# The last 64-token group of an attention and mixer kernel in two column parts, with its stores in parts on both queues

## The chip, the cores and the metric

The kernel runs on one core of a Trainium2 chip. The metric is the device time of one execution in microseconds (us), the median of several runs; less is better. Engines are named as the profile names them: PE is TensorE (PEld its weight loads), DVE is VectorE, ACT is ScalarE, POOL is GpSimd, SP is SyncE, which here only issues transfers; a q behind a name is that engine's instruction queue. A name such as L891 is a line of the kernel before.

## The reference

For each of 8 batches, 12 heads, 448 tokens and head dimension 64, sigmoid attention; its output, heads side by side, is a matrix x of 448 tokens by 768 columns, and goes through a mixer:

```python
scores = scale * np.matmul(q, k.transpose(0, 1, 3, 2)) - np.log(S)
attn = 1.0 / (1.0 + np.exp(-scores))
x = np.matmul(attn, v)                       # then (B, S, H * D)
h = np.maximum(xt @ w_tok1, 0.0) @ w_tok2    # xt: x with tokens last
u = x + h.transpose(0, 2, 1)
h2 = np.maximum(u @ w_ch1, 0.0) @ w_ch2
return u + h2
```

Inputs and output are float32; the kernel computes its products from float16 operands into float32 sums.

## The kernel before

The schedule is written out by hand: instructions go to the engines in the order of the Python code, and waits are put between them where data or buffers demand it. Batches overlap: while the scores and values of one batch are computed, the channel products of the batch before are done in between. At the end only the channel products of batches 6 and 7 are left, and then the last group of batch 7.

Tokens are taken as position p = 0 to 63 and residue j = 0 to 6 (token 7 p + j), so a batch is seven groups of 64 tokens, by residue. Residues 0 to 5 make three pairs of 128 tokens. The seventh residue, 64 tokens, is alone. In the second channel product, `h2` (the hidden values, 12 blocks of 128 channels by 448 tokens) is the stationary operand and `c2` (the weights, 12 blocks of 128 by 768 columns) the moving one; the 768 columns are done as two halves of `DH` = 384.

The pairs of 128 tokens of batches 6 and 7 go through `ch2_seven`: seven products of six matmuls in place of eight (L814), each sum added to an output tile by DVE (L841, three columns blocks of 128 at a time). When a pair is ready, `store` (L621) sends its two 64-token rows, 192 KB each; for batch 7 the first goes out from SP and the second from ACT, for batch 6 both from SP.

The last group is `ch2_last(B - 1)`, called in four portions of three blocks by `pieces_last`. The 64 tokens fill only half of the array's columns, so the two halves of the output columns, g = 0 and 1, are done side by side: g = 0 into partitions 0 to 63 of one PSUM bank, g = 1 into partitions 64 to 127 of another. Twelve pairs of matmuls of 384 columns (L891) are followed by three pairs of 128 columns (L902), which add u: `ut(b, db)` is u with its columns on the partitions, so a matmul with the identity turns it over into the sum. Then DVE copies g = 0 (L914) and ACT copies g = 1 (L912) into the tile `o` of `last_tile`, and each half, 96 KB, is stored by a queue of its own, SP and ACT (L923).

`un[b]` is u with tokens on the partitions, made by a DMA transpose earlier (`utrans`); its 64 partitions of the seventh residue are partitions 0 to 63. `bank` gives one of four PSUM banks by a counter `at_bank` (or by a list in the opening), `two_banks` one of two pairs of banks that the scores use (tag `qk`), which at the end serve the first channel product.

Every transfer that SP or ACT issues counts its completion on one of eight counters; the build hands them out in turn, and before an issue its queue waits until the previous transfer on the same counter has landed. The closing line (L1489) makes SP wait for all counters one after the other in a fixed order, and then the engines meet.

Other lines that the text names: L170 are transposes on PE, pairs of 128-column matmuls into 64 partitions each, as L902's; L544 and L535 are DVE and ACT reading sums of the first channel product from PSUM; L717 are stores of the seventh group of earlier batches, 96 KB each.

Of the kernel before, what the change touches and what calls it, by code (L numbers as in the profile page):

```python
# [10 lines left out]
FP32 = mybir.dt.float32  # L11
ADD = mybir.AluOpType.add
# [4 lines left out]
COPYF = mybir.ActivationFunctionType.Copy  # L17
# [4 lines left out]
NJ = 7  # L22
NP = 64
NU = 3
NS = 224
BY_GROUP = [0, 1, 6, 7, 2, 3, 8, 9, 4, 5, 10, 11]
# [4 lines left out]
def kernel(  # L31
# [11 lines left out]
    nc = tc.nc  # L43

    B, H, S, E = q.shape
# [4 lines left out]
    NCB = CC // 128  # L50
    N_CYCLES = NU * B
    N_FIRST = 4
    DH = D // 2
# [10 lines left out]
    ident = pc.tile([128, 128], FP16, name="ident")  # L64
# [4 lines left out]
    c2 = pc.tile([128, NCB, D], FP16, name="c2")  # L69
# [11 lines left out]
    def xu(b):  # L81
        return xus[b % 2] if b else xu_0
# [3 lines left out]
    at_bank = [0]  # L86

    def bank(shape, dtype, name):

        if opening_banks:  # L90
            n = opening_banks.pop(0)
        else:
            n = at_bank[0]
            at_bank[0] = (n + 1) % 4
        return pp.tile(shape, dtype, tag=f"m{n}", bufs=1, name=name)

    raw, rel, tr = {}, {}, {}
    att, xn, h1, un = {}, {}, {}, {}
# [4 lines left out]
    def raw_tile(b, t):  # L103
        if (b, t) not in raw:
            tag, bufs = f"raw_{t}", 2 if t == "v" else 1
            if b == 1 and t != "v":
                tag = f"rel_{t}"
            raw[b, t] = pa.tile(
                [128, NU, 2, NJ, E], FP16, tag=tag, bufs=bufs, name=f"raw_{t}_{b}"
            )  # L110
        return raw[b, t]
# [92 lines left out]
    def two_banks(name):  # L204
        ps = pp.tile([128, 2, 512], FP32, tag="qk", bufs=2, name=name)
        return [ps[:, n, :] for n in range(2)]
# [141 lines left out]
    h2 = {}  # L348

    acc = {}  # L350
# [3 lines left out]
    def ut(b, db):  # L354
        return xu(b)[:, db % NU, db // NU, :]
# [198 lines left out]
    orow = out.rearrange("b (p j) d -> b j p d", j=NJ)  # L554
# [18 lines left out]
    def last_tile(b):  # L573
        return pa.tile([128, DH], FP32, tag="outl", bufs=1, name=f"o_{b}_3")
# [302 lines left out]
        return turns[0], lambda: turn_over(jobs[1][0]), turns[1], end  # L877

    def ch2_last(b, n0=0, n1=NCB):
        final = b == B - 1  # L880
        if n0 == 0:
            acc[b] = [
                bank([128, 512], FP32, f"c2_{b}_3_{g}")
                for g in range(2 if final else 1)
            ]
        parts = [slice(0, 64), slice(64, 128)]
        ps = [acc[b][g if final else 0][parts[g], 0:DH] for g in range(2)]
        add_on_pe = final or b not in un
        for n in range(n0, n1):
            for g in range(2):  # L890
                nc.tensor.matmul(  # L891
                    out=ps[g],
                    lhsT=h2[b][:, BY_GROUP[n], 384:448],
                    rhs=c2[:, BY_GROUP[n], DH * g : DH * g + DH],
                    start=(n == 0),
                    stop=(n == NCB - 1 and not add_on_pe),
                )
        if n1 < NCB:
            return
        for n in range(NU if add_on_pe else 0):  # L900
            for g in range(2):
                nc.tensor.matmul(  # L902
                    out=ps[g][:, 128 * n : 128 * n + 128],
                    lhsT=ut(b, NU * g + n)[:, 384:448],
                    rhs=ident[:, :],
                    start=False,
                    stop=(n == NU - 1),
                )
        o = last_tile(b)
        for g in range(2):  # L910
            if final and g == 1:
                nc.scalar.activation(out=o[parts[g], :], in_=ps[g], func=COPYF)  # L912
            elif add_on_pe:
                nc.vector.tensor_copy(out=o[parts[g], :], in_=ps[g])  # L914
            else:
                nc.vector.tensor_tensor(
                    out=o[parts[g], :].rearrange("s (u d) -> s u d", d=128),
                    in0=un[b][0:64, :, g, 3, :],
                    in1=ps[g].rearrange("s (u d) -> s u d", d=128),
                    op=ADD,  # L920
                )
            queue = nc.scalar if final and g == 1 else nc.sync
            queue.dma_start(  # L923
                out=orow[b, NJ - 1][:, DH * g : DH * g + DH], in_=o[parts[g], :]
            )


    for g, queue in enumerate((nc.scalar, nc.sync)):
        queue.dma_start(
            out=first_q[64 * g : 64 * g + 64].rearrange("p hi j e -> p hi (j e)"),  # L930
            in_=q[0, 6 * g : 6 * g + 2].rearrange("h (p j) e -> p h (j e)", j=NJ),
# [27 lines left out]
    for par in range(2):  # L959
        part = slice(64 * par, 64 * par + 64)  # L960
        nc.gpsimd.dma_start(
            out=w1[part, 0:3, :],
            in_=tok_rows[0:6].rearrange("(t par) p c -> par p t c", par=2)[par],
# [4 lines left out]
        out=w2s[:, :, :], in_=moe_w_tok2.rearrange("(tc t) s -> t tc s", tc=2)  # L968
# [45 lines left out]
    def pieces_last(b):  # L1014
        for n in range(0, NCB, 3):
            yield 3 * DH, lambda n=n: ch2_last(b, n, n + 3)
# [9 lines left out]
    def keep_warm(n):  # L1026
# [16 lines left out]
        out=raw_tile(0, "q")[:, 0, :, 4:NJ, :], in_=first_q[:, :, 4:NJ, :], func=COPYF  # L1043
# [102 lines left out]
    for c, cb in ((N_FIRST, 3), (N_FIRST + 1, 8)):  # L1146
        b, u = divmod(c, NU)
# [73 lines left out]
    for c in range(2 * NU, ONE_RUN):  # L1221
        b, u = divmod(c, NU)
# [74 lines left out]
    X, Y = 2, 0  # L1297
# [95 lines left out]
    for c in range(ONE_RUN, N_CYCLES):  # L1393
        b, u = divmod(c, NU)
# [63 lines left out]
    both.plain(3)  # L1458
    seven.plain(4)
    both.plain(4)  # L1460
    at_bank[0] = Y + 1
    for w, f in pieces_last(B - 1):
        f()


# [28 lines left out]
```

## Time and profile before

| | |
|---|---|
| median of 3 runs | 340.45 us (340.07 to 340.86) |
| profiled execution, its time | 341.39 us |
| profiled execution, span from first to last instruction | 339.6 us |
| granted TensorE clock, mean | 0.998 |
| PE, DVE, ACT, POOL busy, share of the span | 98%, 69%, 63%, 17% |
| last L902 matmul, start of the last stores on ACT and SP | 334.80 + 0.33, 335.71, 335.74 us |

The busy share of an engine counts its instructions from start to end; matmuls are pipelined, so successive ones overlap in it. Times such as 335.71 are microseconds from the start of the span. A row of the timeline gives the start, the time from the first start to the last end of the instructions merged in it, the engine, the line, what is written and read, and their count; in brackets stands the idle time ahead of it and who ended it. A row of the groups by line gives the busy time and the mean of one in ns. A row of the DMA issues ends with the KB of one issue and the microseconds from issue to landing.

### The profile page before, as it was taken

The numbers are of one execution on the slowest core, as the hardware profiler recorded it, in microseconds if no ns is written. First come the engines' busy times: TensorE is split into PE (matmuls) and PEld (weight loads), VectorE is DVE, ScalarE is ACT, GpSimd is POOL, SyncE is SP. The second block draws the span as 40 slices with busy tenths as digits, with TensorE's granted clock in tenths as the row PEclk, the third lists the DMA queues.
The fourth block names the chain that finished last, engine by engine and source line by source line (L and its number), as shares of the span: only waits on it lengthen the run. The fifth ranks groups of instructions, "written<-read, shape, count | busy, mean of one in ns | idle before, by whom it ended". The sixth has DMA issues, their size and how long they took to land.

```text
span 339.6 us, 10285 instructions
## 1 busy us (share of the span) xinstructions
PE 332.2 (98%) x4423; PEld 242.5 (71%) x4423; DVE 234.9 (69%) x484; ACT 213.0 (63%) x272; POOL 58.7 (17%) x102
## 2 busy tenths in 40 slices
PE   7999999999999999999999999999999999999994
PEld 4555565555796679866896679866896679769852
DVE  2277366678998973877768773878758654876882
ACT  3997657388647895578647895578647795314200
POOL 8981550050031000220032002020010000000000
PEclk9999999999999999999999999999999999999999
DMA  7999999999999999998999899988995293028007
GB/s 119 173 174 195 206 205 204 163 175 237 169 187 189 140 168 211 185 142 161 204 145 172 138 206 175 206 117 134 196 175 93 56 193 73 2 56 185 4 11 197
DMA packets 104381, 52.17 MB, mean 154 GB/s; under 512 B 76432, under 2 KB 101264, under 8 KB 104336
## 3 DMA queue, kind: packets, MB, share of 16 engines
q1 hardware_dynamic: 78704, 29.11, 47.8%
q0 software_dynamic: 25168, 21.50, 42.1%
q10 hardware_dynamic: 464, 0.92, 1.0%
q8 instruction: 34, 0.56, 0.7%
q14 instruction: 11, 0.09, 0.1%
HBM read 43.45 MB, written 11.01 MB: 160 GB/s over the span
## 4 chain that ended last, share of the span: by engine, by line
PE 86%; DMA 5%; POOL 4%; ACT 2%; issue 1%; DVE 0%; ACTq 0%; POOLq 0%
PE c_ab L514 14%; PE c L814 10%; PE qk L187 9%; PE c_c L514 8%; PE xa L218 7%; PE c L861 6%; PE tk L296 5%; PE yt L316 5%; PE c L387 4%; DMA c<-in_moe_w_ch_dram 4%; PE c L584 4%; PE c L364 3%; PE c L669 3%; PE c L650 2%; ACT att L194 2%; DMA raw_v<-in_v_dram 2%
## 5 line engine op out<-in xcount | busy, mean ns | idle before, releaser
L194 ACT ACTIVATE att<-qk,att_bias 128x896 f16<-128x896 f32 x168 | 156.0, 1012 | 38.6 <-PE qk L187 37.6
L187 PE MATMUL qk<-tr_q,tr_k 64*64 64x448 f16 x672 | 61.3, 360 | 0.3 <-ACT att L194 0.2
L514 PEld LDWEIGHTS <-c 128*128 128x128 f16 x504 | 48.4, 98 | 1.1 <-issue 0.3
L218 PE MATMUL xa<-att,raw_v 64*64 64x448 f16 x644 | 40.7, 349 | 0.0
L187 PEld LDWEIGHTS <-tr_k 64*64 64x64 f16 x672 | 25.2, 105 | 19.0 <-issue 11.9
L514 PEld LDWEIGHTS <-sum 128*128 128x128 f16 x378 | 36.3, 98 | 0.0
L227 DVE CAST xu<-xa 128x448 f16<-128x448 f32 x40 | 23.1, 619 | 18.8 <-PE xa L218 18.4
L535 ACT ACTIVATE pt_ab<-c_ab 128x896 f32<-128x896 f32 x21 | 19.2, 917 | 20.6 <-PE c_ab L514 20.6
L218 PEld LDWEIGHTS <-raw_v 64*64 64x64 f16 x672 | 22.0, 107 | 8.3 <-issue 0.4
L861 PE MATMUL c<-c,h 64*64 64x384 f16 x360 | 24.6, 322 | 0.0
L1127 POOL COPY gate<-tr_q 128x2 f16<-128x2 f16 x6 | 1.6, 275 | 121.7 <-DMA tr_q<-rel_q 121.7
L326 DVE TENSOR_TENSOR xu<-xu,yt 128x448 f16<-128x448 f16 x38 | 21.7, 613 | 0.0
L537 ACT ACTIVATE h<-c_ab 128x896 f16<-128x896 f32 x7 | 6.4, 917 | 24.4 <-PE c_ab L514 24.4
L296 PE MATMUL tk<-xn,w 128*128 128x256 f16 x156 | 21.2, 274 | 0.1
L544 DVE TENSOR_TENSOR h<-pt_ab,c_ab 128x896 f16<-128x896 f32 x14 | 15.2, 1084 | 8.6 <-PE c_ab L514 8.6
L544 DVE TENSOR_TENSOR h<-pt_c,c_c 128x448 f16<-128x448 f32 x21 | 12.9, 614 | 11.7 <-PE c_c L514 11.6
L316 PE MATMUL yt<-w,h 128*128 128x448 f16 x88 | 20.3, 353 | 0.0
L841 DVE TENSOR_TENSOR o<-un,c 128x384 f32<-128x384 f16 x32 | 17.4, 550 | 4.0 <-PE c L814 4.0
L310 ACT ACTIVATE h<-tk 128x256 f16<-128x256 f32 x42 | 14.2, 406 | 9.5 <-PE tk L296 9.5
L814 PEld LDWEIGHTS <-hid 128*128 128x128 f16 x132 | 12.9, 98 | 8.0
L514 PE MATMUL c_ab<-diffs,c 128*128 128x224 f16 x168 | 18.4, 259 | 0.0
L296 PEld LDWEIGHTS <-w 128*128 128x128 f16 x156 | 13.6, 98 | 5.7 <-issue 2.4
(134 smaller groups left out, 572.1 us busy)
## 6 DMA issues: line engine op xcount, KB each, us to landing
out_dram<-o SPq DMA_DIRECT2D x41, 192.0 KB, 3.2
c<-in_moe_w_ch_dram POOLq DMA_DIRECT2D x4, 1152.0 KB, 16.1
raw_k<-in_k_dram POOLq DMA_DIRECT2D x10, 336.0 KB, 6.9
raw_q<-in_q_dram POOLq DMA_DIRECT2D x10, 336.0 KB, 5.7
raw_v<-in_v_dram POOLq DMA_DIRECT2D x10, 336.0 KB, 8.8
out_dram<-o SPq DMA_DIRECT2D x15, 96.0 KB, 2.4
raw_q<-in_q_dram POOLq DMA_DIRECT2D x12, 112.0 KB, 5.1
raw_k<-in_k_dram POOLq DMA_DIRECT2D x12, 112.0 KB, 5.4
```

The lines of the kernel that those rows point to most:

```text
L187: nc.tensor.matmul(out=ps[64 * g : 64 * g + 64, hi, 0:S], lhsT=tr[b, "k"][64 * hi : 64 * hi + 64, u, j, 64 * g : 64 * g + 64], rhs=tr[b, " ...
L194: nc.scalar.activation(out=att[b, u, j][:, :, :], in_=ps[:, :, 0:S], func=SIGMOID, bias=bias_t[:, :], scale=att_scale,)
L218: nc.tensor.matmul(out=ps[g][64 * hi : 64 * hi + 64, 0:S], lhsT=raw[b, "v"][64 * g : 64 * g + 64, u, hi, j, :], rhs=att[b, u, j][64 * g : ...
L227: nc.vector.tensor_copy(out=xu(b)[:, u, g, 0:S], in_=ps[g][:, 0:S])
L296: nc.tensor.matmul(out=ps[tcb], lhsT=w1[rows, t, cols], rhs=xn[b, u][rows, :, t, :], start=(t == 0 and not with_scores), stop=(t == (2 if ...
L316: nc.tensor.matmul(out=ps[:, 0:S], lhsT=h1[b, u][:, tcb, g, :], rhs=w2[:, tcb, :, :], start=(tcb == 0), stop=(tcb == 1),)
L326: nc.vector.tensor_tensor(out=x, in0=x, in1=ps[:, 0:S], op=ADD)
L514: nc.tensor.matmul(out=ps[:, g, p, :], lhsT=weights[n][:, d, 128 * cb : 128 * cb + 128], rhs=moving[n][:, d, :], start=(n in (1, 5, 2) and ...
L535: nc.scalar.activation(out=shaped(part[:, :, :]), in_=ps, func=COPYF)
L544: nc.vector.tensor_tensor(out=shaped(dst), in0=shaped(parts[gs, which]), in1=ps, op=ADD)
L814: nc.tensor.matmul(out=ps[:, 0:DH], lhsT=self.weights[n][:, k, :], rhs=self.moving[n][:, k, :], start=(n in (1, 2, 5) and k == 0), stop=(k ...
L861: nc.tensor.matmul(out=ps[m : m + 64, 0:DH], lhsT=lhsT(n)[part, m : m + 64], rhs=rhs(n)[part, :], start=(opens and turn == 0 and n == 0), ...
```

## The change

The last group of batch 7 leaves `ch2_last` (which stays for batch 0, with one bank and with u added by PE as before) and goes to a new function, `ch2_end`. It takes the 384 columns of each half in two parts, 256 and then 128, each part into a pair of score banks from `two_banks`. In each part, twelve pairs of matmuls come first; then PE adds u for g = 1 alone, two matmuls of 128 columns in the first part and one in the second. For g = 0 DVE adds `un` to the sum while it moves it to `o`; ACT copies g = 1. Then the part is stored, g = 0 from SP and g = 1 from ACT: 64 KB each in the first part, 32 KB each in the second.

```diff
-    at_bank[0] = Y + 1
-    for w, f in pieces_last(B - 1):
-        f()
+    ch2_end(B - 1)
...
+    def ch2_end(b):
+        o = last_tile(b)
+        for u0, u1 in ((0, 2), (2, 3)):
+            banks = two_banks(f"c2_{b}_3_{u0}")
+            width = 128 * (u1 - u0)
+            ps = [banks[g][64 * g : 64 * g + 64, 0:width] for g in range(2)]
+            for n in range(NCB):
+                for g in range(2):
+                    at = DH * g + 128 * u0
+                    nc.tensor.matmul(
+                        out=ps[g],
+                        lhsT=h2[b][:, BY_GROUP[n], 384:448],
+                        rhs=c2[:, BY_GROUP[n], at : at + width],
+                        start=(n == 0),
+                        stop=(g == 0 and n == NCB - 1),
+                    )
+            for u in range(u0, u1):
+                nc.tensor.matmul(
+                    out=ps[1][:, 128 * (u - u0) : 128 * (u - u0) + 128],
+                    lhsT=ut(b, NU + u)[:, 384:448],
+                    rhs=ident[:, :],
+                    start=False,
+                    stop=(u == u1 - 1),
+                )
+            cols = slice(128 * u0, 128 * u1)
+            nc.vector.tensor_tensor(
+                out=o[0:64, cols].rearrange("s (u d) -> s u d", d=128),
+                in0=un[b][0:64, u0:u1, 0, 3, :],
+                in1=ps[0].rearrange("s (u d) -> s u d", d=128),
+                op=ADD,
+            )
+            nc.scalar.activation(out=o[64:128, cols], in_=ps[1], func=COPYF)
+            for g, queue in enumerate((nc.sync, nc.scalar)):
+                queue.dma_start(
+                    out=orow[b, NJ - 1][:, DH * g + 128 * u0 : DH * g + 128 * u1],
+                    in_=o[64 * g : 64 * g + 64, cols],
+                )
```

In `ch2_last` the branches for the last batch go: one bank in place of two, PE always adds u, DVE makes both copies, both stores go out from SP.

More of the change, by code (lines that the diff above doesn't have):

```diff
@@ L879, in ch2_last @@
     def ch2_last(b, n0=0, n1=NCB):
-        final = b == B - 1
         if n0 == 0:
[L882 to L885, printed above, removed]
+            acc[b] = bank([128, 512], FP32, f"c2_{b}_3")
         parts = [slice(0, 64), slice(64, 128)]
-        ps = [acc[b][g if final else 0][parts[g], 0:DH] for g in range(2)]
-        add_on_pe = final or b not in un
+        ps = [acc[b][parts[g], 0:DH] for g in range(2)]
         for n in range(n0, n1):
@@ L895, in ch2_last @@
                     start=(n == 0),
-                    stop=(n == NCB - 1 and not add_on_pe),
+                    stop=False,
                 )
@@ L899, in ch2_last @@
             return
-        for n in range(NU if add_on_pe else 0):
+        for n in range(NU):
             for g in range(2):
@@ L910, in ch2_last @@
         for g in range(2):
[L911 to L921, printed above, removed]
@@ L922, in ch2_last @@
-            queue = nc.scalar if final and g == 1 else nc.sync
-            queue.dma_start(
+            nc.vector.tensor_copy(out=o[parts[g], :], in_=ps[g])
+            nc.sync.dma_start(
                 out=orow[b, NJ - 1][:, DH * g : DH * g + DH], in_=o[parts[g], :]
             )
+    def ch2_end(b):
[35 more added lines that the diff above has]
+                )
```

## Prediction

> **What bounds the kernel now.** I read the page first. TensorE is busy for nearly all of the span, so the time moves only by matmul work, or by what stands behind the last matmul.
>
> ```profile
> span 339.6 us, 10285 instructions
> PE 332.2 (98%) x4423; PEld 242.5 (71%) x4423; DVE 234.9 (69%) x484; ACT 213.0 (63%) x272; POOL 58.7 (17%) x102
> ```
>
> As built, the instruction lists of the two kernels agree on every engine up to the last token group. Whatever the change does happens in the last 7 us. There I read the timeline from 332.8 us on, and the chain of waits for the same stretch.
>
> ```profile
> 332.54 1.48 ACTq L621 DMA_DIRECT2D out_dram<-o  x2
> 332.76 1.84 SPq L621 DMA_DIRECT2D out_dram<-o  x2
> 332.82 2.14 PE L891 MATMUL c<-c,h 128*64 128x384 f16 x24
> 334.80 0.33 PE L902 MATMUL c<-ident,xu 128*64 128x128 f16 x6
> 335.17 0.55 DVE L914 COPY o<-c 64x384 f32<-64x384 f32 x1 [1.68 <-PE c L902]
> 335.20 0.49 ACT L912 ACTIVATE o<-c 64x384 f32<-64x384 f32 x1 [15.38 <-PE c L902]
> 335.71 0.50 ACTq L923 DMA_DIRECT2D out_dram<-o  x1
> 335.74 0.47 SPq L923 DMA_DIRECT2D out_dram<-o  x1
> ```
>
> ```profile
> 332.89 2.07 PE c L891 x24
> 334.96 0.21 PE c L902 x6
> 335.18 0.54 DVE o L914
> ```
>
> The chain is plain: matmuls to 335.13, the two copies side by side to 335.72 and 335.69, two stores. After the issue of the stores nothing computes, yet the span runs to 339.6. The view of DMA issues says where 2.6 us of the last 3.9 go, and the instructions of the closing line (L1489) on SP show the rest.
>
> ```profile
> out_dram<-o ACTq DMA_DIRECT2D x1, 96.0 KB, 2.6
> out_dram<-o SPq DMA_DIRECT2D x1, 96.0 KB, 2.4
> ```
>
> ```profile
> L1489 SPq EVENT_SEMAPHORE  x7: 28/28/28, 338.3 to 338.7; - x7
> ```
>
> ACT's store lands last, at 335.71 + 2.6 = 338.31. SP then walks the remaining completion counters one after the other, seven waits from 338.3 to 338.7, some 0.065 us apart, and the closing exchange between the engines ends the span 1.29 us behind the landing. The profiled execution took 341.39 us, 1.8 us more than its span; the median shown is 340.45 us, 0.94 us below it. I make the sum on the span and take the difference over to the median.
>
> **The matmuls.** The first L891 matmul of the group waits in the old build for the banks' earlier readers (L841), and in the new one not; those readers had ended before 332.8 (the L841 copy at 332.93 reads another bank), so nobody stood there and I put the move to the score banks at nothing. It could save at most the 0.09 us by which the first matmul is later than its predecessors' pitch.
>
> ```profile
> 332.57 0.33 PE L814 MATMUL c<-hsum_b,h 128*128 128x384 f16 x1
> L902 PE MATMUL c<-ident,xu 128*64 128x128 f16 x6 | 0.3, 219 | 0.0
> 58.45 0.56 PE L170 MATMUL tp_q<-ident,raw_q 128*64 128x128 f16 x14
> ```
>
> The two halves' matmuls run in pairs, one on each half of the array's columns. A pair of 384 columns takes (2.14 - 0.33)/11 = 0.164 us. A pair of 128 columns takes, by the transposes of L170 (seven pairs in 0.56, the last lasting 0.22), 0.34/6 = 0.057 us. The middle, 0.110, is my estimate for 256 columns, with 0.27 for one. Removed: 12 x 0.164 + 3 x 0.057 = 2.14. Added: 12 x 0.110 + 2 x 0.057, then 12 x 0.057 + 0.057, together 2.18. The three adds of u that VectorE takes over were halves of pairs whose other half stays, so they give TensorE nothing back; 42 instructions more cost 0.04 us, and the last matmul ends at 335.15 to 335.17.
> [...]
>
> **What is handed over earlier.** The pairs start at 332.82: the first part's sums for VectorE end at 332.82 + 11 x 0.110 + 0.27 = 334.30, its u for ScalarE at 334.42, the second part's at 335.10 and 335.15. From the end of the matmul to the copy the trace has 0.04 us on VectorE, 0.07 on ScalarE. Their durations by width:
>
> ```profile
> L841 DVE TENSOR_TENSOR o<-un,c 128x384 f32<-128x384 f16 x32 | 17.4, 550 | 4.0 <-PE c L814 4.0
> L544 DVE TENSOR_TENSOR h<-pt_ab,c_ab 128x896 f16<-128x896 f32 x14 | 15.2, 1084 | 8.6 <-PE c_ab L514 8.6
> L535 ACT ACTIVATE pt_ab<-c_ab 128x896 f32<-128x896 f32 x21 | 19.2, 917 | 20.6 <-PE c_ab L514 20.6
> L535 ACT ACTIVATE pt_c<-c_c 128x448 f32<-128x448 f32 x21 | 11.3, 544 | 7.7 <-PE c_c L514 7.7
> ```
>
> VectorE: 534 ns for 512 columns more, so 1.04 ns a column on 150; the add costs as much as the copy did (550 at 384), and 256 columns take 0.42 us, 128 take 0.28. ScalarE: 0.83 ns a column on 170; 0.38 and 0.28.
> - SP: VectorE 334.34 to 334.76, store of 64 KB issued at 334.78 (SP's earlier stores end at 332.76 + 1.84 = 334.60), 0.47 us, free at 335.25. VectorE again 335.14 to 335.42. Store of 32 KB ready at 335.44, where 96 KB were issued at 335.74.
> - ACT: copy 334.49 to 334.87, issue 334.90 to 335.40. That issue stands ahead of the second copy on ScalarE's own queue, which could else begin at 335.22. So 335.42 to 335.70, and the 32 KB store goes at 335.72: no earlier than the 335.71 of before.
>
> **The wait that it adds.** Each store counts its completion on one of eight counters taken in turn, and its issue first waits for the previous transfer on that counter. Two stores more turn this wheel on by two. By the built waits SP's last store shares the counter of ACT's L621 store of 332.54, whose landing is late:
>
> ```profile
> out_dram<-o ACTq DMA_DIRECT2D x1, 192.0 KB, 3.4
> ...
> L923 SPq EVENT_SEMAPHORE  x1: 17/17/17, 334.7 to 334.7; - x1
> L923 ACTq EVENT_SEMAPHORE  x1: 17/17/17, 335.2 to 335.2; - x1
> ```
>
> 332.54 + 3.4 = 335.94; SP goes on at about 335.99, 0.25 us later than its single store of before. In the old kernel the same kind of wait took 17 ns on either queue. Behind SP's wait there stands only the closing list, which waits for that store anyhow. ACT's second store shares a counter that is free by 334.3, the two first parts likewise.
>
> **How long the stores take.** The engine share of the transfers (second column from the right) in the last stretches, then three stores' times to landing: two of 96 KB at 298.3, and the 192 KB that SP and ACT issue at 333.5.
>
> ```profile
> 335.50:336.00 0.50, 0.00 (x0) 0.00 (x0) 0.21 (x1) 0.18 (x1) 0.00 (x0) 1.00 1.06 381
> 336.00:336.50 0.50, 0.00 (x0) 0.00 (x0) 0.00 (x0) 0.00 (x0) 0.00 (x0) 1.00 1.01 381
> 336.50:337.00 0.50, 0.00 (x0) 0.00 (x0) 0.00 (x0) 0.00 (x0) 0.00 (x0) 1.00 0.90 353
> 337.00:337.50 0.50, 0.00 (x0) 0.00 (x0) 0.00 (x0) 0.00 (x0) 0.00 (x0) 1.00 0.93 267
> 337.50:338.00 0.50, 0.00 (x0) 0.00 (x0) 0.00 (x0) 0.00 (x0) 0.00 (x0) 1.00 0.32 105
> ```
>
> ```profile
> out_dram<-o SPq DMA_DIRECT2D x2, 96.0 KB, 2.2
> ```
>
> ```profile
> out_dram<-o SPq DMA_DIRECT2D x1, 192.0 KB, 4.1
> out_dram<-o ACTq DMA_DIRECT2D x1, 192.0 KB, 3.9
> ```
>
> The engines are full until 337, moving the stores of the two groups before, and the last 192 KB follow directly. Early 64 KB parts therefore mostly stand in line: they fill the 0.1 to 0.2 that 336.5 to 337.5 leaves idle, and the last bytes move perhaps 0.2 us sooner. No row shows 32 KB. The nearest are 2.2 and, on these queues, 2.4 and 2.6; below, the smaller size may take 0.1 off the 2.2, above, a full line gives 4.1. I take 2.1 for SP, which starts last into engines that are running dry, and 2.3 for ACT, and keep 2.0 to 2.6 for the range.
> [...]
>
> **The sum.** SP's last store lands at 335.99 + 2.1 = 338.09, ACT's at 335.72 + 2.3 = 338.02, against 338.31. SP's is now the last, and its counter is the fifth of the eight in the closing list, where ACT's was the second: three of the waits that followed the landing are over by then, 3 x 0.065 = 0.2 us. So 338.09 + 1.29 - 0.2 = 339.18 for the span against 339.6, a gain of 0.4 us, 0.12%. The median goes from 340.45 to 340.05. With landings of 2.0 and 2.6 the span is 339.1 and 339.7: 339.95 to 340.55 from the costs alone, to which the scatter of the three runs shown, 0.4 us to either side, adds.
>
> **The rivals.** About 0.2%, 0.7 us, is what a measurement of this kernel can tell from no change.
> - No gain at all: the bytes are the same, they go through the same engines, and the closing stretch follows the last of them. Then the gain from the shorter copies is swallowed by the counter wait and the line, and the landing comes at 338.3 to 338.5; with the shorter closing walk the span is 339.4 to 339.6, the median 340.25 to 340.45. The full engine share until 337 speaks for it, the drop to 0.32 behind 337.5 against it. [...] To a measurement this is the same as the forecast.
> - The counter wait binds less than I say and the line is short: ACT's L621 store lands by 335.4, SP issues at 335.46, and both last parts land 2.0 us behind their issue, at 337.46 and 337.72. ACT's counter is the fourth, so 337.72 + 1.29 - 0.13 = 338.9: a gain of 0.7 us, a median of 339.7. This is about all that can be had, since ACT's issue does not move. The 3.4 us of the L621 store speak against it.
> - Slower: the wait and the line add up. SP's 32 KB go out last, at 335.99, behind everything on both queues; should four stores in pieces clog the engines so that this one takes as long as the 192 KB stores at 333.5, it lands at 335.99 + 4.1 = 340.1, the span is 341.2, the median 342.0. It turns into a measurable loss once the time to landing exceeds 339.6 + 0.7 - 1.09 - 335.99 = 3.2 us. Against it: nothing is issued behind it, and the two single stores of before took 2.4 and 2.6 in the same line.
> That the change does not do what it says is no case of its own: the built order shows two parts, the adds on VectorE, and stores on both queues.
>
> **How the numbers follow.** The forecast, a gain of 0.2 to 0.65 us, has 0.52; no gain, with a loss of up to 0.7 us from costs not seen, 0.24; the large gain 0.16; the loss 0.08. Same is 0.52 + 0.24 = 0.76, faster 0.16, slower 0.08. The range is 339.6 to 340.75: below it lies half of the large gain, above it the loss; the cases of no gain end at 340.45 and scatter reaches 0.3 beyond.
>
> **What would show it.** Right: SP's 64 KB store near 334.8 and its 32 KB store near 336.0, with a wait row in between that ends at the landing of ACT's store of 332.5; ACT's second store near 335.7; PE's last matmul within 0.1 us of before; last landing near 338.1 on SP. Wrong: SP's second store near 335.45 (the counter does not bind), a last landing at or behind 338.3 (the line does), matmul pairs of the second part well over 0.06 us apart, or a difference anywhere ahead of 332.8 us.

## The result, and the profile after

The changed kernel takes 342.52 us (median of 13 runs) against 340.86 us for the kernel before (13 runs): the ratio is 1.0053, with a 95% interval of 1.0035 to 1.0071. It is slower by about 1.7 us, where 0.4 us less was forecast. Ratios and their intervals, here and below, are estimated from all executions but those in a slower state of the chip, so they differ a little from the ratio of two medians.

The profiled execution took 341.78 us, its span is 340.0 us. From the page of the kernel after, its span, TensorE's rows and the row of the instruction queue (blocks, MB, share of the transfer engines' time):

```profile
span 340.0 us, 10333 instructions
...
PE 330.6 (97%) x4444; PEld 242.4 (71%) x4444; DVE 235.0 (69%) x485; ACT 213.1 (63%) x273; POOL 58.5 (17%) x102
...
q8 instruction: 35, 0.57, 0.6%
```

and the same row of the kernel before:

```profile
q8 instruction: 34, 0.56, 0.7%
```

One block more of instructions was fetched. The spans alone, 340.0 and 339.6, hide what it did, because the work ahead of the last group ends at different times from run to run: the first matmul of the last group stood at 332.82 in the profile before and at 331.73 here, and between 331.4 and 336.8 in all profiles of this study. What the change touches is the stretch from that matmul to the end of the span: 6.79 us before (332.82 to 339.62), 8.27 us after, 1.48 us more. This stretch is called the tail below. The timeline of the kernel after in it:

```profile
331.73 1.55 PE L921 MATMUL c<-c,h 128*64 128x256 f16 x25
...
333.18 0.84 PE L921 MATMUL c<-c,h 128*64 128x128 f16 x22
333.38 0.41 DVE L937 TENSOR_TENSOR o<-un,c 64x256 f32<-64x256 f16 x1 [0.99 <-PE c L929]
333.82 1.69 SPq L945 DMA_DIRECT2D out_dram<-o  x2
333.83 0.38 ACT L943 ACTIVATE o<-c 64x256 f32<-64x256 f32 x1 [15.10 <-DVE o L937]
333.85 0.22 PE L929 MATMUL c<-ident,xu 128*64 128x128 f16 x1
334.11 0.28 DVE L937 TENSOR_TENSOR o<-un,c 64x128 f32<-64x128 f16 x1 [0.32 <-PE c L929]
334.24 0.47 ACTq L945 DMA_DIRECT2D out_dram<-o  x1
334.75 0.27 ACT L943 ACTIVATE o<-c 64x128 f32<-64x128 f32 x1 [0.55 <-DVE o L937]
335.06 0.82 ACTq L945 DMA_DIRECT2D out_dram<-o  x1
```

TensorE takes 2.34 us in place of 2.31, as worked out. Counted from the first matmul, SP's second store is issued at 3.31 us (335.04) and ACT's at 3.33, where the single stores of before went at 2.92 and 2.89. ScalarE's row names VectorE's add as what it waited for. The DMA issues of the four parts, SP and ACT in turn, 64 KB and then 32 KB:

```profile
out_dram<-o SPq DMA_DIRECT2D x1, 64.0 KB, 4.4
out_dram<-o ACTq DMA_DIRECT2D x1, 64.0 KB, 4.2
out_dram<-o SPq DMA_DIRECT2D x1, 32.0 KB, 3.6
out_dram<-o ACTq DMA_DIRECT2D x1, 32.0 KB, 3.8
```

32 KB take longer to land than the 96 KB of before (2.4 and 2.6). The engine share of the transfers says why (second column from the right); below it stands the row of the instruction queue in the stretch 335.21 to 336.10.

```profile
335.00:335.50 0.50, 0.00 (x0) 0.00 (x0) 0.00 (x0) 0.03 (x1) 0.00 (x0) 1.00 1.05 383
335.50:336.00 0.50, 0.00 (x0) 0.00 (x0) 0.00 (x0) 0.00 (x0) 0.00 (x0) 1.00 0.87 307
336.00:336.50 0.50, 0.00 (x0) 0.00 (x0) 0.00 (x0) 0.00 (x0) 0.00 (x0) 1.00 0.85 246
336.50:337.00 0.50, 0.00 (x0) 0.00 (x0) 0.00 (x0) 0.00 (x0) 0.00 (x0) 1.00 0.38 105
337.00:337.50 0.50, 0.00 (x0) 0.00 (x0) 0.00 (x0) 0.00 (x0) 0.00 (x0) 1.00 0.05 20
337.50:338.00 0.50, 0.00 (x0) 0.00 (x0) 0.00 (x0) 0.00 (x0) 0.00 (x0) 1.00 0.07 23
```

```profile
q8 instruction: 1, 0.02, 6.2%
```

From 337.0 to 338.0 the share is 0.05 to 0.07: about one engine of sixteen (0.0625) works alone. The trace records sixteen landings for each store. Of the last store's, fifteen are in by 337.47 and the sixteenth comes at 338.84; on the three other part stores it is the same, 1.3 us between the fifteenth and the sixteenth. From 335.24 on a single transfer of 16 KB of instructions occupied one engine for 0.88 us: 6.2% of sixteen engines, a sixteenth, for the whole stretch. The reading is that what this engine still had in line of the stores came late, and the closing list waits for all sixteen (the span ends 1.16 us behind the last sixteenth landing); the experiments test it.

The page before counts 4423 matmuls and as many weight loads, 8846 instructions of TensorE, and 34 blocks on this queue: as an estimate from these two, should the blocks be TensorE's list, 260 instructions a block. The changed kernel has 8888 instructions of TensorE and 35 blocks.

### The profile page after: what moved, and what is told of

It is laid out like the page before. It is cut to its first block, busy times and chain, and to the rows that moved or that the text cites. A ratio compares the mean times of both kernels' runs of the same rounds, so it can differ in the third digit from the quotient of the medians.

```text
span 340.0 us, 10333 instructions
## 1 busy us (share of the span) xinstructions
PE 330.6 (97%) x4444; PEld 242.4 (71%) x4444; DVE 235.0 (69%) x485; ACT 213.1 (63%) x273; POOL 58.5 (17%) x102
## 4 chain that ended last, share of the span: by engine, by line
PE 86%; DMA 5%; POOL 4%; ACT 2%; issue 1%; ACTq 0%; DVE 0%; POOLq 0%
PE c_ab L514 14%; PE c L814 10%; PE qk L187 9%; PE c_c L514 8%; PE xa L218 7%; PE c L861 6%; PE tk L296 5%; PE yt L316 5%; PE c L387 4%; PE c L584 4%; DMA c<-in_moe_w_ch_dram 3%; PE c L364 3%; PE c L669 3%; PE c L650 2%; ACT att L194 2%; DMA w2s<-in_moe_w_tok_dram 2%
```

## The experiments

**Theories.** F: TensorE's list, 42 instructions longer, asks for a 35th block of instructions at a moment when the last stores are in line, and the engine that brings it holds them up. P: the pieces themselves cost, four stores of 64 and 32 KB in a full line. O: chance or the opening makes the difference. Since the work ahead of the last group scatters by more than the effects, each experiment is judged by its tail in the profile, one execution of each kernel, and the times stand beside it.

**1. The kernel before with as many instructions as the changed one.**

```diff
     keep_warm(16)
+    for _ in range(21):
+        nc.tensor.matmul(
+            out=heat[0][:, 0:64],
+            lhsT=warm[:, 0:128],
+            rhs=warm[:, 0:64],
+            start=True,
+            stop=True,
+        )
```

> The kernel before, unchanged in its last group, with 21 short matmuls more (64 columns each) behind the opening's sixteen warming matmuls, where TensorE waits for its first operand anyway; TensorE's list is as long as the changed kernel's (42 instructions more). Theory F (instruction fetch): TensorE's list is fetched in 16 KB blocks, and the longer list asks for a 35th block, whose 0.9 us occupy one transfer engine while the last stores run; then a 35th block shows near the end, one of the sixteen landings of the last stores comes about 1.2 us after the other fifteen, and the time is 1.0 to 1.6 us over the kernel before. Theory P (pieces): the loss comes from four small stores in a full line; then this kernel is as the kernel before, within 0.4 us.

341.50 us, ratio 1.0026 (1.0003 to 1.0049); tail 7.05 us. The 35th block is there, with the last group as it was before. But it came 1.53 us behind the group's first matmul, where in the changed kernel it came at 3.5 us, and cost 0.1 to 0.3 us of tail instead of 1.0 to 1.6:

```profile
331.45 2.14 PE L891 MATMUL c<-c,h 128*64 128x384 f16 x24
```

```profile
q8 instruction: 1, 0.02, 0.8%
...
out_dram<-o ACTq DMA_DIRECT2D x1, 96.0 KB, 2.9
out_dram<-o SPq DMA_DIRECT2D x1, 96.0 KB, 2.6
```

The stores land in 2.9 and 2.6 in place of 2.6 and 2.4. So the size that F gave was a miss: a block more is not enough. That the moment counts was the guess that followed. P, within 0.4 us of the kernel before, is left open by it: the medians differ by 0.64 us, and the interval reaches from 0.1 to 1.7. F was sharpened to the moment for experiments 5 and 6.

**2 and 3. The changed kernel with a short list, and its control.** Both kernels get the same opening: 16 warming matmuls of 512 columns in place of 37 of 256, which is 42 instructions fewer.

```diff
-                out=heat[0][:, 0:256],
+                out=heat[0][:, 0:512],
...
-    keep_warm(16)
+    keep_warm(7)
...
```

> The changed kernel with its last group as it is, and 42 TensorE instructions fewer in the opening: 16 warming matmuls of 512 columns in place of 37 of 256, so TensorE's list is as long as that of the kernel before. Theory F: 34 blocks, no late sixteenth landing, last landing 1.3 us sooner against the last matmul than in the changed kernel; time 0 to 0.5 us under the kernel before, apart from what the opening does. Theory P: as the changed kernel, 1.2 to 1.8 us over the kernel before. A third theory, O, that the opening or chance upstream makes the difference: then this kernel and its control differ from the kernel before by the same amount.

> Control for the opening: the kernel before with the same 16 warming matmuls of 512 columns in place of 37 of 256, last group unchanged. Theories F and P: as the kernel before within 0.4 us, 34 blocks. Theory O: its difference from the kernel before is that of the short-listed changed kernel.

Changed: 341.54 us, ratio to the kernel before 1.003 (1.0005 to 1.0055), tail 6.82 us. Control: 341.95 us, 1.0033 (1.0011 to 1.0056), tail 6.94. The opening itself costs something, against the control's expectation, and the intervals are too wide to tell the two apart. The tail is clear: with 34 blocks and the same last group it falls from 8.27 to 6.82. Of the first, the page's row, the start of the last group (the span ends at 342.70) and the last part stores:

```profile
q8 instruction: 34, 0.56, 0.6%
```

```profile
335.88 1.55 PE L921 MATMUL c<-c,h 128*64 128x256 f16 x25
```

```profile
out_dram<-o SPq DMA_DIRECT2D x1, 32.0 KB, 2.3
out_dram<-o ACTq DMA_DIRECT2D x1, 32.0 KB, 2.3
```

P would have kept the landings at 3.6 and 3.8. It falls as the cause of the 1.5 us. But no gain appears either: 6.82 against 6.79 and 6.94, where the prediction's sum makes 339.18 - 332.82 = 6.36. Experiments 7 to 10 look for that.

**4. The changed kernel again.** No edit.

> The changed kernel again, on the chip of the others. Theory F: 35th block within 1 us of the end of the matmuls in every profile, 8.0 to 8.4 us from the first matmul of the last group to the end, 1.2 to 1.8 us over the kernel before. Theory O (chance upstream): under 0.7 us over it.

342.41 us, ratio 1.0036 (1.0014 to 1.0058), 1.4 us over the 341.03 us of the kernel before on that chip. Its tail is 8.22 us; the block came 3.36 us behind the first matmul, 1.0 us behind the end of the last, for 0.92 us. Its row from 335.75 to 336.70, and the last part stores:

```profile
q8 instruction: 1, 0.02, 6.1%
...
out_dram<-o SPq DMA_DIRECT2D x1, 32.0 KB, 3.7
out_dram<-o ACTq DMA_DIRECT2D x1, 32.0 KB, 3.7
```

The effect repeats, on the chip on which experiments 5, 6 and 8 ran without it, and O falls.

**5 and 6. The block earlier.** 116 instructions more in the opening of both kernels: the 21 short matmuls of experiment 1, and

```diff
-        for _ in range(n):
+        for _ in range(2 * n):
...
-                out=heat[0][:, 0:256],
+                out=heat[0][:, 0:128],
...
```

> The changed kernel with 116 TensorE instructions more in the opening (each warming matmul of 256 columns as two of 128, and 21 short ones where TensorE waits for its first operand). Theory F, in its sharper form: not the number of blocks costs, but the moment. The list still takes a 35th block, but it is asked for 116 instructions earlier, some 5 to 8 us before the end of the matmuls' last group, ahead of most of the last stores; so the loss goes: from the first matmul of the last group to the end of the span 6.8 to 7.1 us as without the block (changed kernel 8.27), time 1.0 to 1.6 us under the changed kernel. Theory P, or a theory that any 35th block costs: 8.0 to 8.4 us, time as the changed kernel.

> Control: the kernel before with the same longer opening. From the first matmul of the last group to the end 6.8 to 7.0 us (kernel before 6.79), a 35th block earlier than the last group; time within 0.4 us of the kernel before, unless the opening itself costs. The difference between this and the changed kernel with the same opening is then that of the last group alone: theory F says within 0.3 us of zero.

Changed: tail 6.83 us, 342.45 us, ratio 1.0032 (1.0005 to 1.006). Control: tail 6.98 us, 341.84 us, ratio 1.0023 (0.9998 to 1.0047). Still 35 blocks, but in the changed kernel the last begins at 330.6, 3.3 us ahead of the group's first matmul. That matmul, the page's row, the row from 330.55 to 331.60 and the last part stores:

```profile
333.91 1.55 PE L921 MATMUL c<-c,h 128*64 128x256 f16 x25
```

```profile
q8 instruction: 35, 0.57, 0.7%
```

```profile
q8 instruction: 1, 0.02, 5.2%
```

```profile
out_dram<-o SPq DMA_DIRECT2D x1, 32.0 KB, 2.3
out_dram<-o ACTq DMA_DIRECT2D x1, 32.0 KB, 2.4
```

Same last group, same count of blocks as the changed kernel, and the 1.4 us are gone from the tail. The whole time does not show it: the forecast 1.0 to 1.6 us under the changed kernel was a miss, the medians being equal, since this opening costs too (its control is 0.8 us over the kernel before). The pair itself differs by 0.6 us in the medians, where within 0.3 was expected; its intervals overlap, so what is left may be scatter.

**7. PSUM tiles of their own.** On top of experiment 2:

```diff
-            banks = two_banks(f"c2_{b}_3_{u0}")
+            if u0 == 0:
+                banks = [two_banks(f"c2_{b}_3_{u0}_{g}")[g] for g in range(2)]
+            else:
+                at_bank[0] = Y + 1
+                banks = [bank([128, 512], FP32, f"c2_{b}_3_{u0}_{g}") for g in range(2)]
```

> The short-listed changed kernel, with a PSUM tile of its own for each half in each part (first part in one bank of each score pair, second part in two of the single banks), so that ScalarE's copies wait for TensorE and not for VectorE's add. In the changed kernel ScalarE's first copy started 0.44 us after its sums were ready, behind VectorE. Theory F: ScalarE's first store goes out 0.4 us earlier, its second 0.3 to 0.4; what is left is SP's wait for the counter of an earlier store, so the time is 0 to 0.3 us under the short-listed changed kernel. Theory P: as the changed kernel within 0.4 us.

341.12 us, ratio 1.0019 (0.9993 to 1.0044); tail 6.77 us. ScalarE now waits for TensorE:

```profile
333.78 0.38 ACT L947 ACTIVATE o<-c 64x256 f32<-64x256 f32 x1 [14.65 <-PE c L933]
```

```profile
out_dram<-o ACTq DMA_DIRECT2D x1, 32.0 KB, 2.6
out_dram<-o SPq DMA_DIRECT2D x1, 32.0 KB, 2.6
```

Its first copy starts 1.65 us behind the first matmul (2.10 in the changed kernel), its last store goes at 2.88 (3.33) and SP's at 3.13. But both take 2.6 us to land in place of 2.3: what was issued sooner waited longer, and the tail stays within 0.05 us of experiment 2's. The median is 0.4 us lower, more than the 0 to 0.3 expected; the intervals overlap.

**8. One part.** The loop runs once, over 384 columns:

```diff
-        for u0, u1 in ((0, 2), (2, 3)):
+        for u0, u1 in ((0, 3),):
```

> The changed kernel with one part of 384 columns in place of two: score banks and VectorE's add as in the change, but a single store of 96 KB for each half. TensorE's list is 6 instructions shorter than before's, so there is no 35th block. ScalarE's copy waits for VectorE's add, as both read one PSUM tile: its store goes out 0.5 us later than in the kernel before, SP's at the same time. Theory F: from the first matmul of the last group to the end 6.9 to 7.3 us, 0.1 to 0.5 us over the kernel before. If the two readers of one tile do not matter: 6.8.

340.84 us against 341.03, ratio 0.9995 (0.997 to 1.0019); tail 6.76 us, 34 blocks. ScalarE's store goes 0.55 us later than in the kernel before, as expected, and the tail is not longer for it, against the 6.9 to 7.3 us forecast: that store lands in 2.1 us where 2.6 stood before, and SP's, issued at the same 2.92 us behind the first matmul, in 2.1 where 2.4 stood.

```profile
out_dram<-o SPq DMA_DIRECT2D x1, 96.0 KB, 2.1
out_dram<-o ACTq DMA_DIRECT2D x1, 96.0 KB, 2.1
```

**9. Parts in the copies and stores only.** The products in one part, each half in a bank of its own, then

```diff
+        for u0, u1 in ((0, 2), (2, 3)):
             cols = slice(128 * u0, 128 * u1)
...
-                in1=ps[0].rearrange("s (u d) -> s u d", d=128),
+                in1=ps[0][:, cols].rearrange("s (u d) -> s u d", d=128),
...
```

> The changed kernel with the products in one part of 384 columns, each half in a single PSUM bank of its own, and only the copies and the stores in the two parts (256, 128); TensorE's list 6 instructions shorter than before's, so no 35th block. The sums are ready at once, so ScalarE's second copy again waits for its first store's issue, and SP's second store goes out at about 336.1 on the clock of the kernel before. The bytes in line are the same. Line theory: 6.7 to 7.0 us from the first matmul of the last group to the end, time within 0.4 us of the kernel before. If small parts in themselves pay: under 6.6.

341.06 us against 341.00, ratio 1.0002 (0.9983 to 1.0022); tail 6.81 us, with landings of 2.3 and 2.1 us for the last parts. No version tried beats the kernel before; this one and those of experiments 7 and 8 cannot be told from it.

**10. The line ahead taken out.** The two 192 KB stores of batch 7's last pair are left out of both kernels:

```diff
-            if n in (3, 4):
+            if n in (3, 4) and (b, t) != (B - 1, 2):
                 store(b, t)
```

> The short-listed changed kernel with own PSUM tiles, leaving out the two 192 KB stores of the last 128-token pair of batch 7 (those rows of the output are not written). It takes the transfers out that stand in line just ahead of the last group's. If the line is what swallowed the gain of the pieces: first matmul of the last group to the end about 6.1 us (last store on ACT 2.9 us behind that matmul, landing 2.1, closing 1.1), which is 0.2 to 0.3 us under the kernel before with the same stores left out. If the pieces bring nothing even so: equal to that one within 0.1 us.

> Control: the kernel before without the same two stores. Line theory: 6.3 to 6.4 us from the first matmul of the last group to the end, against 6.8 to 7.0 with them; its stores land within 2.1 to 2.3 us, against 2.4 to 2.8.

Changed: tail 5.97 us, 340.63 us, ratio to the kernel before 0.9996 (0.997 to 1.0023). Control: tail 6.41 us, 340.40 us, ratio 0.9975 (0.9955 to 0.9995). Their last stores, first of the changed, then of the control:

```profile
out_dram<-o SPq DMA_DIRECT2D x1, 32.0 KB, 1.9
out_dram<-o ACTq DMA_DIRECT2D x1, 32.0 KB, 1.8
```

```profile
out_dram<-o ACTq DMA_DIRECT2D x1, 96.0 KB, 2.4
out_dram<-o SPq DMA_DIRECT2D x1, 96.0 KB, 2.1
```

With those two stores out of the line, the tail with the pieces is 0.44 us shorter, more than the 0.2 to 0.3 expected. It is one profile of each, and the whole times do not show it: the medians of eight executions lie the other way, within their scatter, and the two openings differ. ACT's last store shows the line best: issued 2.88 us behind the first matmul in experiment 7 and here, it lands in 2.6 us there and in 1.8 here. With the line, the eight kernels without a late block (the kernel before and its two controls, experiments 2, 5, 7, 8 and 9) lie between 6.76 and 6.98 us, whatever the pieces, the banks and the order. (Taking out the two stores also moved the last stores to other counters; SP's second store did not have to wait here, 2.58 us behind the first matmul in place of 3.13. For SP's store the two effects were not parted.)

## Why the prediction was wrong

The forecast was a gain of 0.12%; the result is a loss of 0.53%, and 342.52 us stand against a range of 339.6 to 340.75. Of the 2.5 us between the 340.05 us forecast and that, 0.4 us is the start: the kernel before measured 340.86 us over 13 runs, and the sum began at 340.45.

- The step that failed first is in the part on the matmuls: "42 instructions more cost 0.04 us". That is what they cost on TensorE, 2.34 against 2.31 us. Their fetch was not in the sum at all. It cost 1.4 us: the tail of 8.27 and 8.22 us with the late block, 6.82 without it and 6.83 with it moved ahead. The page of the kernel before held the row with 34 blocks, and the prediction did not read it.
- The loss is not that of the slower rival. It had the place right, a last 32 KB store taking far longer than 2.1 us, and even the point from which it decides, 3.2 us (3.6 and 3.8 were measured). It had the mechanism wrong: the pieces did not clog the engines (without the late block the last of them landed in 2.3 us), one block of instructions held one engine (0.88 us). That its 342.0 us lies close to the measured 342.52 is luck.
- The pair costs held: 0.057 us for a pair of 128 columns, (0.84 - 0.22)/11 = 0.056 measured (the 22 matmuls of that row are ten pairs and, at the end, two single ones, 11 steps). The copy times held: 0.41, 0.28 on VectorE, 0.38, 0.27 on ScalarE.
- "From the end of the matmul to the copy" was wrong for ScalarE. Both halves' sums of one part are in one PSUM tile, and the build makes ScalarE's copy wait for VectorE's add; this stood in the built order and was overlooked. First copy 2.10 us behind the first matmul in place of 1.67, last store 3.33 in place of 2.90. VectorE's first add, too, began 0.13 us later than worked out, behind the first part's matmuls of u, which it does not need.
- The counter wait is there: ACT's 192 KB store on the same counter landed at 3.25 us behind the first matmul and SP's second store went at 3.31, where 3.17 was worked out. In experiment 2, without the late block, it went at 3.17.
- The landings of 2.1 us for SP and 2.3 for ACT were too short for a full line: 2.3 and 2.3 without the block, 2.6 and 2.6 when ScalarE was freed, and 1.9 and 1.8 only with two stores of the line taken out. In all, 32 KB on SP's and ACT's queues took 1.8 to 2.6 us without a late block. So the rival "no gain at all" was right on what is left of the change: swallowed, as far as experiments 7 and 10 show it, by the line. Tails of 6.76 to 6.98 us followed, whichever way the same bytes were cut.
- The shorter closing walk held: 340.0 - 338.84 = 1.16 us behind the landing, where 1.29 stood before; 0.13 less for ACT's counter.

The traces tell in part where in the list the 35th block is asked for. Counted in matmuls and weight loads of TensorE that have started, its transfer begins after 8865 of them in experiment 5, after 8867 in experiment 6 and after 8870 in experiment 1. The kernel before has 8846 in all and never gets there; the changed one has 8888. It passes the 8865th at 1.73 us behind the first matmul of the last group, yet its block's transfer begins only at 3.51 us (3.36 in the repeat). That the block itself stood in line behind the stores is likely, but not shown.

In experiment 1, where the block came at 1.53 us, the lag of the sixteenth landing behind the fifteenth shrinks: 0.6 us on the two 192 KB stores of the last pair, 0.1 on the two last stores. In the changed kernel it stays at 1.2 to 1.4 us on the same two and the four part stores (1.1 to 1.3 in the repeat). What stays open is why it does not shrink there, and why it is longer than the 0.88 us that the block took.

## What to carry to other kernels

Count the instructions that an edit adds to an engine's list, and look at the row of the instruction queue: near the end of a program a block more of code can land among the last stores and, as here, cost more (1.4 us) than the edit was to win (0.4 us). Where the transfer engines are as full ahead of the last landings as they were here (0.90 to 1.06 from 335.5 to 337.5 us in the kernel before), cutting or advancing the last stores can move the wait from the issue to the landing, as in experiment 7 against experiment 2 (ACT's last store issued 0.45 us sooner, landing in 2.6 us in place of 2.3); look at the engine share ahead of the last store before pricing a smaller one. And where the work ahead scatters by more than the effect, compare the stretch that the edit touches, from its first instruction to the end, and check the built waits of every instruction in it.

## What the runs showed of the hardware

A block of 16 KB of instructions went over one transfer engine (6.2% of sixteen while it lasted), in 0.88 to 0.92 us for the late ones here. That it shared this engine with the stores is the reading of their landings: in the changed kernel the sixteenth landing of the six last stores came 1.2 to 1.4 us behind the fifteenth, in the kernel before 0.09 to 0.13 us on the four last. A store's issue on SP's or ACT's queue took 0.47 to 0.50 us in the last group of the kernel before, though the two overlapped (335.71 and 335.74); of the four issues of the changed kernel two took 0.88 and 0.82 us. What lengthened them was not tested.
